# Attention ahead of two expert networks: scores of two heads on the two row halves of TensorE, loads in 4 KB rows, decay on values and result

## The chip, the cores and the metric

The kernel runs on one core of one Trainium2 chip. The metric is the device time of one execution in microseconds (us), less is better. Before the change it was 1580.83 us, the median of three runs (1585.57, 1577.12 and 1580.83).

## What is computed

Three stages follow each other. The first, the only one that the change touches, is a causal attention whose weights decay with distance instead of passing a softmax. The second sends each of the 4608 tokens to one of 8 experts, the third is a dense network.

```python
# q, k, v: (B, H, S, D) = (8, 8, 576, 64), float32
gamma = 1.0 - 2.0 ** (-5.0 - np.arange(H))
rel = pos[:, None] - pos[None, :]
Dmat = np.where(rel >= 0, gamma[:, None, None] ** rel[None], 0.0)
ret = (q @ k.transpose(0, 1, 3, 2)) / np.sqrt(D) * Dmat[None]
x = (ret @ v)                      # -> (B*S, H*D) = (4608, 512)
x = moe(x, ...)                    # argmax over 8 experts, 512 -> 1024 -> 512
out = mlp(x, ...)                  # 512 -> 2048 -> 512, h - tanh(h)
```

The decay gamma^(i-j) is a product of a part of the query's place, gamma^i, and a part of the key's place, gamma^(-j). That is what both versions build on, each in its own way.

## The kernel before

The 4608 tokens are 36 tiles of 128 (`TL`). A sequence has 576 tokens, so 9 tiles (`PERIOD`) hold two sequences and the fifth tile of each nine (t % 9 == 4) holds the end of one and the start of the next, 64 tokens each. All work of one tile is emitted in one pass of a loop over t (L531 on); every engine then runs its own list in that order, and waits by semaphores.

For tile t the pieces are:

- `load_group` (L247): q, k and v of two tiles at once (`LG = 2`), five transfers on SP's queue: the transposed keys `kpad` in two halves of 64 partitions (L255, L256), with each head's half beside zeros, the transposed queries `qt` (L257), the values `vn` (L258) and the keys again, untransposed, `kn` (L259). In memory a partition's row of a tile pair is 1 KB for each head pair of `kT` and `qT`, and 2 KB for each tile of `vN` and `kN`. The buffers hold two groups. A group is ordered two groups ahead, at odd t, once its buffers are free.
- `scores` (L310), emitted for t+1 ahead of `attend` of t: eight matmuls (L318) give the scores of 8 heads; each uses all 128 rows, since the zeros in `kpad` blot out the other head of the pair. VectorE (DVE) multiplies them by a table of decay and causality, `d_full` (L320), into `a`, in two halves of four heads. In the mixed tile GpSimd (POOL) sets a quarter of `a` to zero (L323).
- `scaled` (L326), emitted for t+2: POOL multiplies the queries by gamma^i, `qq` (L331), and the keys by gamma^(-j), `kk` (L335).
- `attend` (L342): `xp` = running state times `qq` (four matmuls, L354) plus `vn` times `a` (eight matmuls on two column halves, L362); then the state in `st` is raised by `kk` times `vn` (eight, column halves, L377). DVE copies one half of the state to `sdiag`, ScalarE (ACT) the other (L383).
- `evac_x` (L386): ACT copies `xp` to `xt` (L390).
- Between these stand, for the group of four tiles before, `route_a`, `route_b` and `route_c` (L417, L426, L448; the routing's logits, argmax and ranks), `scatter` (POOL's indirect writes, L476), and `store_x` (four transposes on TensorE, L487, a scaling on ACT, L492, and a write to `x_d` on ACT's queue).
- `filler` (L507): one of 28 steps that turn seven float64 weight tiles of the third stage to float32 pairs (`conv`, L168, mostly on DVE). The weights' next 512 KB load (L173) is issued on SP's queue from such a step, and waits there until DVE has read the one buffer.

The lines that set the order of the loads:

```python
if t % LG == LG - 1 and t // LG + 2 < NLG:
    load_group(t // LG + 2)
if t + 4 in (5, 6, 7, 8):
    nc.sync.dma_start(out=qs[:, t + 3], in_=A["qs"][t + 3])
```

When the first 28 tiles are routed, `choose` (L392) picks the expert with most of them, and its first unit of 400 tokens is gathered from `x_d` (L164) while the last tiles run. The expert stage begins with the matmuls of L667, and neither it nor the third stage is changed.

Of the kernel before, what the change touches and what calls it, by code (L numbers as in the profile page):

```python
# [8 lines left out]
F32 = mybir.dt.float32  # L9
# [5 lines left out]
ALU = mybir.AluOpType  # L15
# [6 lines left out]
DM = H * D  # L22
E, FF = 8, 1024
DFF = 2048
TL = 128
NTILE = NT // TL
PERIOD = 9
LG = 2
NLG = NTILE // LG
# [18 lines left out]
# -h(h) for small h:  s = (SQ_A u + SQ_B)^2, (s + SQ_C)(u - SQ_R) u h, u = h^2  # L48
# [4 lines left out]
def _consts():  # L53
    g = (1.0 - 2.0 ** (-5.0 - np.arange(H))).astype(np.float64)
    j = np.arange(TL)[:, None]
    i = np.arange(TL)[None, :]
    low = (j <= i)
    rel = np.where(low, i - j, 0)
    dec = np.where(low[None], g[:, None, None] ** rel[None], 0.0) / 8.0
    d_full = np.ascontiguousarray(dec.transpose(1, 0, 2)).astype(np.float32)  # L60
    qs = np.zeros((PERIOD, 2, H // 2, D, TL))
    ks = np.zeros((TL, PERIOD, H))
    for t in range(PERIOD):
        pos = TL * t + np.arange(TL)
        bb, loc = pos // S, pos % S
        start = bb == (TL * t) // S
        for h in range(H):
            if t % PERIOD:
                qs[t, h % 2, h // 2] = (np.where(start, g[h] ** loc, 0.0) / 8.0)[None, :]
            nxt = bb == (TL * (t + 1) - 1) // S  # L70
            ks[:, t, h] = np.where(nxt, g[h] ** (-loc.astype(np.float64)), 0.0)
    qs = np.ascontiguousarray(qs.transpose(0, 1, 3, 2, 4).reshape(PERIOD, 128, H // 2, TL))
    return {
        "d_full": d_full,
        "qs": np.ascontiguousarray(qs[1:]).astype(np.float32), "ks": ks.astype(np.float32),
    }


def _layout(inputs):
    q, k, v = inputs["q"], inputs["k"], inputs["v"]  # L80

    def tr(a):
        a = a.transpose(1, 3, 0, 2).reshape(H // 2, 128, NLG, LG * TL)
        return np.ascontiguousarray(a.transpose(2, 1, 0, 3))

    def tok(a):
        a = a.transpose(0, 2, 1, 3).reshape(NLG, LG, TL, DM)
        return np.ascontiguousarray(a.transpose(0, 2, 1, 3))
# [7 lines left out]
        "qT": tr(q), "kT": tr(k), "kN": tok(k), "vN": tok(v),  # L96
# [11 lines left out]
def kernel(tc, A, out):  # L108
    nc = tc.nc
    with ExitStack() as ctx:  # L110
# [33 lines left out]
        def turn_rows(u, s, src, tp):  # L144
            """Tile s of a unit's rows to a pair of float32r, features on the partitions."""
# [61 lines left out]
        with tc.manual_schedule():  # L207
            make_identity(nc, ident)
            # attention's own buffers on the left; what the routing needs, which ends later, on the right
# [4 lines left out]
            gld = p1("gld", 2)  # L214
# [10 lines left out]
            d_full = att.tile([128, H, TL], F32, name="d_full")  # L225
            qs = att.tile([128, PERIOD - 1, H // 2, TL], F32, name="qs")
            ks = att.tile([128, PERIOD, H], F32, name="ks")
            sdiag = [att.tile([128, H // 2, 128], F32, name=f"sdiag{i}") for i in range(2)]
            wg = const.tile([128, KD, 32], F32, name="wg")
            kpad = [att.tile([128, H // 2, 2, LG * TL], F32, name=f"kpad{i}") for i in range(2)]  # L230
# [14 lines left out]
            gt = {}  # L245

            def load_group(g, parts=1):  # L247
                kp = kpad[g % 2]
                qt = gld.tile([128, H // 2, LG * TL], F32, name="qt")
                vn = gld.tile([128, LG, DM], F32, name="vn")  # L250
                kn = gld.tile([128, LG, DM], F32, name="kn")
                for i in range(parts):
                    c = slice(i * LG * TL // parts, (i + 1) * LG * TL // parts)
                    r = slice(i * LG // parts, (i + 1) * LG // parts)
# [5 lines left out]
                gt[g] = (kp, qt, kn, vn)  # L260

            for i, eng in enumerate((nc.vector, nc.gpsimd)):
                eng.memset(kpad[i][0:64, :, 1, :], 0.0)
                eng.memset(kpad[i][64:128, :, 0, :], 0.0)
# [3 lines left out]
            load_group(0, LG)  # L268
            for i in range(2):
                nc.scalar.dma_start(out=d_full[:, 4 * i:4 * i + 4], in_=A["d_full"][:, 4 * i:4 * i + 4])  # L270
            nc.scalar.dma_start(out=ks, in_=A["ks"])
            nc.scalar.dma_start(out=wg[:, :, 0:E], in_=A["wg"])
            for t in (1, 2):
                nc.sync.dma_start(out=qs[:, t - 1], in_=A["qs"][t - 1])
            nc.scalar.dma_start(out=mid, in_=A["ids"].bitcast(I32).rearrange("p (t w) -> p t w", w=2))
            nc.scalar.dma_start(out=mb.rearrange("p a e -> p (a e)"), in_=A["mb"].to_broadcast([128, 2 * E]))
            load_group(1, LG)
            for t in (3, 4):
                nc.sync.dma_start(out=qs[:, t - 1], in_=A["qs"][t - 1])

# [26 lines left out]
            a_t, q_t, k_t, s_t, x_ps = {}, {}, {}, {}, {}  # L307
            xt = {}

            def scores(t):  # L310
                kp, qt, kn, vn = gt[t // LG]
                c = slice((t % LG) * TL, (t % LG + 1) * TL)
                a = tmp.tile([128, H, TL], F32, name="a")
# [12 lines left out]
            def scaled(t):  # L326
                kp, qt, kn, vn = gt[t // LG]
                c = slice((t % LG) * TL, (t % LG + 1) * TL)
                if t % PERIOD:
                    qq = tmp.tile([128, H // 2, TL], F32, name="qq")  # L330
                    nc.gpsimd.tensor_tensor(out=qq, in0=qt[:, :, c], in1=qs[:, t % PERIOD - 1], op=ALU.mult)  # L331
                    q_t[t] = qq
                if t % PERIOD != PERIOD - 1:
                    kk = tmp.tile([128, H, D], F32, name="kk")
                    nc.gpsimd.tensor_tensor(  # L335
                        out=kk, in0=kn[:, t % LG].rearrange("p (h d) -> p h d", h=H),
                        in1=ks[:, t % PERIOD].unsqueeze(2).to_broadcast([128, H, D]), op=ALU.mult)
                    k_t[t] = kk
# [3 lines left out]
            def attend(t):  # L342
                kp, qt, kn, vn = gt[t // LG]
                r = t % PERIOD
                xp = ps_x.tile([128, H // 2, TL], F32, name="xp")
                a = a_t.pop(t)
                inter = r != 0
                after = not inter or t == NTILE - 1

                def before():  # L350
                    if inter:
                        ss, qq = s_t.pop(t), q_t.pop(t)
                        for p in range(H // 2):
                            nc.tensor.matmul(out=xp[:, p, :], lhsT=ss[:, p, :], rhs=qq[:, p, :],  # L354
                                             start=not after and p == 0, stop=after, skip_group_check=True)
# [3 lines left out]
                for p in range(H // 2):  # L359
                    for s in range(2):  # L360
                        h = 2 * p + s
                        nc.tensor.matmul(out=xp[64 * s:64 * s + 64, p, :], lhsT=vn[:, t % LG, h * D:(h + 1) * D],  # L362
                                         rhs=a[:, h, :], start=after and p == 0, stop=True,
# [4 lines left out]
                if r != PERIOD - 1:  # L368
                    first = r == 0 or r == PERIOD // 2
# [3 lines left out]
                    kk = k_t.pop(t)  # L373
                    for p in range(H // 2):
                        for s in range(2):
                            h = 2 * p + s
                            nc.tensor.matmul(out=st[64 * s:64 * s + 64, p, :], lhsT=kk[:, h], rhs=vn[:, t % LG, h * D:(h + 1) * D],  # L377
                                             start=first and p == 0, stop=True, skip_group_check=True,
                                             tile_position=(0, 64 * s))
# [614 lines left out]
```

## Time and profile before

| | |
|---|---|
| three runs, us | 1585.57, 1577.12, 1580.83 |
| median, us | 1580.83 |
| profiled execution: span of its instructions, us | 1571.7 |
| median less span, us | 9.1 |
| TensorE busy in the whole span | 1457.5 us, 93% |
| DVE, ACT, POOL busy | 1071.6, 704.5, 286.6 us |

For the profiled execution the profile has only its span; the time of the whole execution is not listed apart, and the 9.1 us stand for what lies around the span.

The span is that of one execution, from the first to the last instruction. "Busy" of TensorE is modelled, since matmuls are pipelined: where they follow without a gap, the distance from the start of one group to the start of the next is the better price. The 40 slices of the page are 39.3 us each; attention ends early in the eighth.

### The profile page before, as it was taken

The page shows a single profiled execution, that of the slowest core. Times are in us where ns is not written, and L with a number is a line of the kernel's source. Part 1 is how long each engine was busy: PE and PEld are TensorE (multiplying, and loading weights), DVE is VectorE, ACT ScalarE, POOL GpSimd, SP SyncE. Part 2 cuts the span into 40 slices and gives each one's busy share as a digit, 9 for nine tenths or more (in the row PEclk, how much of TensorE's full clock was granted, in tenths as well). Part 3 has the DMA queues.
Part 4 walks back from the last instruction along what each step waited for, and adds up shares of the span by engine and source line. Part 5 has one row for each costly group of instructions (what it writes and reads, how often), then busy time and mean ns, then how long its engine had stood idle before and what let it go on. Part 6 is the DMA issues. An engine that isn't in the chain of part 4 may idle for free.

```text
span 1571.7 us, 22138 instructions
## 1 busy us (share of the span) xinstructions
PE 1457.5 (93%) x8171; PEld 1279.0 (81%) x8171; DVE 1071.6 (68%) x1775; ACT 704.5 (45%) x1305; POOL 286.6 (18%) x340
## 2 busy tenths in 40 slices
PE   5777777789999999999998999999999999999996
PEld 5666766689999999999776888888888888888885
DVE  3546654457777776774688777877777787877774
ACT  1212222334343344444566555555555555555552
POOL 5234435311111111111232111111111011111101
PEclk8878988999999999999999999999999999999998
DMA  8897797633323522232201000000001000000000
GB/s 234 222 162 166 183 210 147 167 90 117 104 102 117 197 81 78 96 124 88 77 27 59 23 27 27 28 27 28 28 0 37 18 28 27 28 27 1 28 1 27
DMA packets 71008, 127.90 MB, mean 81 GB/s; under 512 B 18704, under 2 KB 37136, under 8 KB 70896
## 3 DMA queue, kind: packets, MB, share of 16 engines
q1 hardware_dynamic: 54976, 92.09, 22.2%
q0 software_dynamic: 7344, 19.44, 3.7%
q10 hardware_dynamic: 8576, 14.91, 3.2%
q8 instruction: 66, 1.08, 0.3%
q14 instruction: 46, 0.38, 0.1%
HBM read 131.10 MB, written 33.09 MB: 104 GB/s over the span
## 4 chain that ended last, share of the span: by engine, by line
PE 39%; issue 6%; DVE 3%; ACT 1%; POOL 1%; DMA 1%; DVEq 0%; POOLq 0%; ACTq 0%
PE hp L667 20%; PE acc L951 7%; PE acc L952 7%; PE acc L953 7%; DVE xl L932 1%; DVE xl L933 1%; DMA o<-wo_d 1%; ACT xh L922 0%; DVE xh L924 0%; POOL out_dram L964 0%; DVE xl L931 0%; DVE lo L927 0%; POOL woutl L905 0%; ACT xh L929 0%; ACT xl L930 0%
## 5 line engine op out<-in xcount | busy, mean ns | idle before, releaser
L951 PE MATMUL acc<-wouth,hi 128*128 128x512 f32 x576 | 226.2, 393 | 4.6 <-ACT o L961 4.6
L667 PE MATMUL hp<-yh,winh 128*128 128x512 f32 x576 | 226.5, 393 | 1.4 <-DVEq L887 1.4
L953 PE MATMUL acc<-wouth,lo 128*128 128x512 f32 x576 | 226.2, 393 | 1.6 <-DVE lo L927 1.6
L667 PE MATMUL hp<-yl,winh 128*128 128x512 f32 x576 | 226.3, 393 | 0.0
L667 PE MATMUL hp<-yh,winl 128*128 128x512 f32 x576 | 226.3, 393 | 0.0
L952 PE MATMUL acc<-woutl,hi 128*128 128x512 f32 x576 | 226.2, 393 | 0.0
L921 ACT ACTIVATE xh<-hp 128x512 f32<-128x512 f32 x144 | 86.1, 598 | 296.9 <-PE hp L667 280.1
L923 DVE TENSOR_TENSOR xl<-xh,hp 128x512 f32<-128x512 f32 x144 | 99.0, 688 | 160.4 <-ACT xh L922 160.4
L767 ACT ACTIVATE hi<-hp 128x400 fp32r<-128x400 f32 x96 | 48.4, 504 | 229.9 <-PE hp L667 229.7
L932 DVE SCALAR_TENSOR_TENSOR xl<-xh,xl 128x512 f32<-128x512 f32 x144 | 135.8, 943 | 15.4 <-DVE xl L931 0.5
L866 PE MATMUL acc<-hi,wh 128*128 128x400 f32 x384 | 137.7, 358 | 5.4 <-ACT wh L742 4.0
L768 DVE SCALAR_TENSOR_TENSOR lo<-hp,hi 128x400 fp32r<-128x400 f32 x96 | 55.0, 573 | 124.9 <-ACT hi L767 122.7
L318 PE MATMUL sc<-qt,kpad 128*128 128x128 f32 x576 | 87.5, 316 | 53.7 <-DMA qt<-in_qT_dram 52.7
L868 PE MATMUL acc<-hi,wl 128*128 128x400 f32 x384 | 133.5, 348 | 0.0
L667 PE MATMUL hp<-xl,wh 128*128 128x400 f32 x384 | 132.8, 346 | 0.0
L667 PE MATMUL hp<-xh,wl 128*128 128x400 f32 x384 | 132.6, 345 | 0.1
L667 PE MATMUL hp<-xh,wh 128*128 128x400 f32 x384 | 132.1, 344 | 0.4 <-ACT wh L742 0.4
L951 PEld LDWEIGHTS acc<-wouth,hi 128*128 128x128 f32 x576 | 108.8, 189 | 29.1 <-ACT o L961 5.0
L867 PE MATMUL acc<-lo,wh 128*128 128x400 f32 x384 | 132.2, 344 | 0.0
L953 PEld LDWEIGHTS acc<-wouth,lo 128*128 128x128 f32 x576 | 108.8, 189 | 28.3 <-DVE lo L927 5.1
L318 PEld LDWEIGHTS sc<-qt,kpad 128*128 128x128 f32 x576 | 82.4, 228 | 60.4 <-issue 45.4
L667 PEld LDWEIGHTS hp<-yh,winh 128*128 128x128 f32 x576 | 108.3, 188 | 25.8 <-PEq L887 1.7
(174 smaller groups left out, 2865.7 us busy)
## 6 DMA issues: line engine op xcount, KB each, us to landing
raw<-in_w_dram SPq DMA_DIRECT2D x91, 512.0 KB
y_d<-yo SPq DMA_DIRECT2D x12, 800.0 KB
yr<-y_d SPq DMA_DIRECT2D x9, 1024.0 KB
raw<-in_wi_dram SPq DMA_DIRECT2D x16, 512.0 KB
kpad<-in_kT_dram SPq DMA_DIRECT2D x32, 256.0 KB
qt<-in_qT_dram SPq DMA_DIRECT2D x16, 512.0 KB
vn<-in_vN_dram SPq DMA_DIRECT2D x16, 512.0 KB
kn<-in_kN_dram SPq DMA_DIRECT2D x16, 512.0 KB
```

What stands on the lines that cost most here:

```text
L318: nc.tensor.matmul(out=sc[:, i, :], lhsT=kp[:, h // 2, h % 2, c], rhs=qt[:, h // 2, c], start=True, stop=True)
L667: nc.tensor.matmul(out=hp, lhsT=lhs, rhs=rhs, start=j == 0, stop=j == 3 * KD - 1)
L768: nc.vector.scalar_tensor_tensor(out=lo, in0=hp, scalar=0.0, in1=hi.bitcast(F32), op0=ALU.max, op1=ALU.subtract)
L866: nc.tensor.matmul(out=o, lhsT=wh[:, cs], rhs=hi, start=first, stop=False)
L867: nc.tensor.matmul(out=o, lhsT=wh[:, cs], rhs=lo, start=False, stop=False)
L868: nc.tensor.matmul(out=o, lhsT=wl[:, cs], rhs=hi, start=False, stop=last)
L921: nc.scalar.activation(out=u, in_=hp, func=ACTF.Square)
L923: nc.vector.tensor_tensor(out=v, in0=u, in1=hp, op=ALU.mult)
L932: nc.vector.scalar_tensor_tensor(out=v, in0=s, scalar=SQ_C, in1=v, op0=ALU.add, op1=ALU.mult)
L951: nc.tensor.matmul(out=acc[s], lhsT=hi[:, c], rhs=wouth[f], start=first, stop=False)
L952: nc.tensor.matmul(out=acc[s], lhsT=hi[:, c], rhs=woutl[f], start=False, stop=False)
L953: nc.tensor.matmul(out=acc[s], lhsT=lo[:, c], rhs=wouth[f], start=False, stop=last)
```

## The change

The loads are laid out anew: `qk` holds queries and keys of a tile, transposed, in one row of 4 KB for each partition, and `vk` values and keys, also 4 KB. A tile is ordered on its own, four tiles ahead (`AHEAD = 4`, four buffers each). `kpad`, its zeros, `d_full` and `qs` are gone.

The scores of a head pair are two matmuls with 64 rows each, one on the rows 0 to 63 and one on 64 to 127, into two banks. They are multiplied by a mask of ones and zeros that all heads share. The mixed tile has a mask of its own, so POOL's memset is gone. The values are scaled by gamma^(-j) on POOL (`vs`), in every tile; queries and keys are used as loaded. The part gamma^i / 8 is applied as `xp` is read out: on DVE, as a product with the table `gx`, where ACT copied before. Both halves of the state are now copied by ACT. In the mixed tile the matmuls of the state run over half the rows or columns.

```diff
-LG = 2
+AHEAD = 4
@@ loads
-                nc.sync.dma_start(out=kp[0:64, :, 0, c], in_=A["kT"][g, 0:64, :, c])
-                (nc.scalar if g + i == 0 else nc.sync).dma_start(out=kp[64:128, :, 1, c], in_=A["kT"][g, 64:128, :, c])
-                nc.sync.dma_start(out=qt[:, :, c], in_=A["qT"][g, :, :, c])
-                nc.sync.dma_start(out=vn[:, r], in_=A["vN"][g, :, r])
-                nc.sync.dma_start(out=kn[:, r], in_=A["kN"][g, :, r])
+            def load_tile(t):
+                qk = gld.tile([128, 2, H // 2, TL], F32, name="qk")
+                vk = gld.tile([128, 2, DM], F32, name="vk")
+                nc.sync.dma_start(out=qk, in_=A["qk"][t])
+                (nc.scalar if t == 0 else nc.sync).dma_start(out=vk, in_=A["vk"][t])
+            def load_gx(r):
+                nc.sync.dma_start(out=gx[:, r], in_=A["gx"][r])
@@ scores
-                for hf in range(2):
-                    sc = ps_sc.tile([128, 4, TL], F32, name="sc")
-                    for i in range(4):
-                        h = 4 * hf + i
-                        nc.tensor.matmul(out=sc[:, i, :], lhsT=kp[:, h // 2, h % 2, c], rhs=qt[:, h // 2, c],
-                                         start=True, stop=True)
-                    nc.vector.tensor_tensor(out=a[:, 4 * hf:4 * hf + 4], in0=sc, in1=d_full[:, 4 * hf:4 * hf + 4], op=ALU.mult)
-                if t % PERIOD == PERIOD // 2:
-                    nc.gpsimd.memset(a[0:64, :, 64:128], 0.0)
+                sc = [ps_sc.tile([128, H // 2, TL], F32, name="sc") for _ in range(2)]
+                for p in range(H // 2):
+                    for s in range(2):
+                        r64 = slice(64 * s, 64 * s + 64)
+                        nc.tensor.matmul(out=sc[s][:, p, :], lhsT=qk[r64, 1, p, :], rhs=qk[r64, 0, p, :],
+                                         start=True, stop=True, tile_position=(64 * s, 0))
+                m = int(t % PERIOD == PERIOD // 2)
+                for s in range(2):
+                    nc.vector.tensor_tensor(out=a[:, s], in0=sc[s], in1=mask[:, m:m + 1, :].to_broadcast([128, H // 2, TL]), op=ALU.mult)
@@ scaled
-                if t % PERIOD:
-                    nc.gpsimd.tensor_tensor(out=qq, in0=qt[:, :, c], in1=qs[:, t % PERIOD - 1], op=ALU.mult)
-                if t % PERIOD != PERIOD - 1:
-                    nc.gpsimd.tensor_tensor(out=kk, in0=kn[...], in1=ks[...], op=ALU.mult)
+                nc.gpsimd.tensor_tensor(out=vs, in0=vk[:, 0]..., in1=vsc[:, t % PERIOD]..., op=ALU.mult)
@@ attend: state to sdiag
-                        (nc.scalar.copy if s else nc.vector.tensor_copy)(out=ss[r64, :, r64], in_=st[r64])
+                        nc.scalar.copy(out=ss[r64, :, r64], in_=st[r64])
@@ evac_x
-                nc.scalar.copy(out=xt[g][:, :, r * TL:(r + 1) * TL], in_=x_ps.pop(t))
+                nc.vector.tensor_tensor(out=xt[g][:, :, r * TL:(r + 1) * TL], in0=x_ps.pop(t), in1=gx[:, t % PERIOD], op=ALU.mult)
@@ loop over t
-                if t % LG == LG - 1 and t // LG + 2 < NLG:
-                    load_group(t // LG + 2)
+                if t + AHEAD < NTILE:
+                    load_tile(t + AHEAD)
+                if t + 3 < PERIOD:
+                    load_gx(t + 3)
```

SP's queue, from the weight load of pass 7 to that of pass 11, before. Rows are DMA issues in the order of the queue, target<-source and the target's shape:

```order
L173 DMA raw<-in_wi_dram 128x1024
L255 DMA kpad_129<-in_kT_dram 64x4x256
L256 DMA kpad_129<-in_kT_dram 64x4x256
L257 DMA qt<-in_qT_dram 128x1024
L258 DMA vn<-in_vN_dram 128x1024
L259 DMA kn<-in_kN_dram 128x1024
L255 DMA kpad_128<-in_kT_dram 64x4x256
L256 DMA kpad_128<-in_kT_dram 64x4x256
L257 DMA qt<-in_qT_dram 128x1024
L258 DMA vn<-in_vN_dram 128x1024
L259 DMA kn<-in_kN_dram 128x1024
L173 DMA raw<-in_wi_dram 128x1024
```

The same stretch of the queue with the change:

```order
L163 DMA raw<-in_wi_dram 128x1024
L239 DMA qk<-in_qk_dram 128x1024
L240 DMA vk<-in_vk_dram 128x1024
L239 DMA qk<-in_qk_dram 128x1024
L240 DMA vk<-in_vk_dram 128x1024
L239 DMA qk<-in_qk_dram 128x1024
L240 DMA vk<-in_vk_dram 128x1024
L239 DMA qk<-in_qk_dram 128x1024
L240 DMA vk<-in_vk_dram 128x1024
L163 DMA raw<-in_wi_dram 128x1024
```

Ten transfers for four tiles have become eight of 512 KB each. The weight load still stands in the same queue, ahead of the loads of its pass. Those of pass 7 were for the tiles 10 and 11 before, and are for tile 11 now; tile 10 is ordered a pass earlier.

DVE's list in the passes 7 and 8 and at the start of 9, before (`a` is the product for the next tile, `cv_` a step of the weight conversion, `sdiag` the copied half of the state):

```order
L320 TENSOR_TENSOR a<-sc,d_full 128x512 x2
L189 TENSOR_SCALAR cv_m<-cv_m 128x512
L190 SCALAR_TENSOR_TENSOR cv_e<-raw,cv_e 128x512
L383 COPY sdiag_126<-st 64x4x64
L320 TENSOR_TENSOR a<-sc,d_full 128x512 x2
L194 TENSOR_TENSOR cv_a<-cv_a,cv_e 128x512
L195 TENSOR_TENSOR cv_a<-cv_a,cv_m 128x512
L320 TENSOR_TENSOR a<-sc,d_full 128x512 x2
L203 TENSOR_TENSOR winl<-cv_a,winh 128x512
```

DVE's list at the same place with the change:

```order
L303 TENSOR_TENSOR a<-sc,mask 128x512 x2
L179 TENSOR_SCALAR cv_m<-cv_m 128x512
L180 SCALAR_TENSOR_TENSOR cv_e<-raw,cv_e 128x512
L366 TENSOR_TENSOR xt<-xp,gx 128x4x128
L303 TENSOR_TENSOR a<-sc,mask 128x512 x2
L184 TENSOR_TENSOR cv_a<-cv_a,cv_e 128x512
L185 TENSOR_TENSOR cv_a<-cv_a,cv_m 128x512
L366 TENSOR_TENSOR xt<-xp,gx 128x4x128
L303 TENSOR_TENSOR a<-sc,mask 128x512 x2
```

The copy of the half state has left DVE's list. The read-out of `xp` has come in at its place, and it stands in every pass, where the state's copy missed the last tile of each nine.

## Rows read from the trace of the kernel before

**Rows 1.** Page, busy tenths of the whole span in 40 slices of 39.3 us: TensorE, its granted clock, mean busy share of the DMA engines.

```profile
PE   5777777789999999999998999999999999999996
...
PEclk8878988999999999999999999999999999999998
...
DMA  8897797633323522232201000000001000000000
```

**Rows 2.** Busy time by stretch: the stretch, its length, busy us (and number of instructions) of TensorE, its weight loads, DVE, ACT and POOL, then granted clock, share of the 16 DMA engines and GB/s. The first row is attention as a whole.

```profile
9.00:279.00 270.00, 202.16 (x2154) 182.78 (x2153) 138.95 (x296) 61.29 (x119) 109.34 (x129) 0.85 0.83 186
218.83:244.28 25.45, 25.15 (x304) 22.58 (x302) 19.12 (x47) 9.74 (x20) 11.19 (x13) 1.00 1.03 232
151.58:169.40 17.82, 15.88 (x195) 14.01 (x193) 14.64 (x32) 5.94 (x12) 7.88 (x9) 1.00 0.80 143
112.50:117.00 4.50, 4.50 (x28) 4.28 (x29) 1.98 (x3) 0.00 (x0) 0.00 (x0) 0.54 1.08 185
119.50:123.00 3.50, 3.50 (x52) 3.38 (x50) 3.40 (x4) 0.81 (x2) 3.31 (x5) 1.00 0.97 371
```

**Rows 3.** Who waited for whom from 9 to 279 us: engine and line <- releaser: us in total, times, longest.

```profile
POOL kk L335 <- DMA kn<-in_kN_dram: 56.8, 11, 12.6
PE sc L318 <- DMA qt<-in_qT_dram: 45.9, 10, 9.9
PE xp L354 <- ACT sdiag L383: 6.1, 5, 3.0
PE m L487 <- ACT xo L492: 3.7, 1, 3.7
PE m L395 <- ACT xo L492: 2.4, 1, 2.4
```

**Rows 4.** DMA traffic: of 9 to 279 us packets and MB with their sizes, and of the stretch 112.5 to 117 us.

```profile
DMA packets 27695, 50.17 MB, mean 186 GB/s; under 512 B 4412, under 2 KB 15215, under 8 KB 27669
...
DMA packets 555, 0.83 MB, mean 185 GB/s; under 512 B 49, under 2 KB 372, under 8 KB 555
```

**Rows 5.** Timeline of the same stretch, SP's queue: start us, length of the issue, line, transfer.

```profile
111.43 0.33 SPq L257 DMA_DIRECT2D qt<-in_qT_dram  x1
118.02 0.33 SPq L258 DMA_DIRECT2D vn<-in_vN_dram  x1
118.45 0.37 SPq L259 DMA_DIRECT2D kn<-in_kN_dram  x1
```

**Rows 6.** Waits of SP's queue from 9 to 279 us: line <- releaser: us in total, times, longest.

```profile
SPq L173 <- DVE sdiag L383: 45.2, 4, 13.5
SPq L258 <- PE st L377: 34.9, 8, 6.2
SPq L257 <- DMA x_d<-xo: 28.4, 7, 8.3
SPq L173 <- DVE cv_e L190: 22.3, 2, 13.3
```

**Rows 7.** Timeline of TensorE in the stretch without load waits, and at the head and the end of the stage (the last row is the first matmul of the experts): start us, us, what, instructions, [idle before].

```profile
6.77 3.75 PE L318 MATMUL sc<-qt,kpad 128*128 128x128 f32 x16 [6.77 <-DMA qt<-in_qT_dram]
12.79 2.44 PE L318 MATMUL sc<-qt,kpad 128*128 128x128 f32 x16 [2.28 <-DMA qt<-in_qT_dram]
15.16 1.98 PE L362 MATMUL xp<-a,vn 128*64 128x128 f32 x16
...
218.83 1.95 PE L318 MATMUL sc<-qt,kpad 128*128 128x128 f32 x16
...
236.19 1.09 PE L362 MATMUL xp<-a,vn 128*64 128x128 f32 x16
237.12 0.64 PE L377 MATMUL st<-vn,kk 128*64 128x64 f32 x16
...
238.17 0.60 PE L487 MATMUL m<-ident,xt 128*128 128x128 f32 x4
238.61 1.95 PE L318 MATMUL sc<-qt,kpad 128*128 128x128 f32 x16
240.40 1.06 PE L354 MATMUL xp<-qq,sdiag 128*128 128x128 f32 x8
...
278.82 1.16 PE L354 MATMUL xp<-qq,sdiag 128*128 128x128 f32 x8
...
292.58 0.45 PE L667 MATMUL hp<-xh,wh 128*128 128x400 f32 x1 [0.37 <-ACT wh L742]
```

**Rows 8.** Groups by line from 9 to 279 us: line, engine, operation, out<-in, shapes, count | busy us, mean ns of one | idle before.

```profile
L320 DVE TENSOR_TENSOR a<-sc,d_full 128x512 f32<-128x512 f32 x72 | 48.3, 685 | 87.6 <-PE sc L318 87.2
L331 POOL TENSOR_TENSOR qq<-qt,qs 128x512 f32<-128x512 f32 x32 | 41.2, 1287 | 67.7 <-DMA qt<-in_qT_dram 51.4 <-PE xp L354 9.3 <-DMA qs<-in_qs_dram 6.6
L335 POOL TENSOR_TENSOR kk<-kn,ks 128x512 f32<-128x512 f32 x32 | 33.5, 1047 | 82.1 <-DMA kn<-in_kN_dram 56.8 <-PE sc L318 18.9 <-PE st L377 6.4
L390 ACT COPY xt<-xp 128x512 f32<-128x512 f32 x35 | 20.5, 585 | 14.5 <-PE xp L362 13.7
L383 DVE COPY sdiag<-st 64x256 f32<-64x256 f32 x32 | 13.2, 414 | 31.6 <-PE st L377 29.6 <-POOL kk L335 1.8 <-issue 0.3
L383 ACT COPY sdiag<-st 64x256 f32<-64x256 f32 x32 | 11.7, 367 | 128.4 <-DVE sdiag L383 124.1 <-DVE cv_m L184 3.4 <-ACT xo L492 0.8
```

**Rows 9.** One line's instructions from 218 to 244 us: engine, operation, duration in ns min/median/max.

```profile
L318 PEld LDWEIGHTS sc<-qt,kpad x80: 186/192/193, 218.7 to 240.2; 128*128 128x128 f32 x80
L318 PE MATMUL sc<-qt,kpad x80: 274/275/377, 218.8 to 240.3; 128*128 128x128 f32 x80
```

More of the change, by code (lines that the diff above doesn't have):

```diff
@@ L56, in _consts @@
     i = np.arange(TL)[None, :]
[L57 to L67, printed above, removed]
-            if t % PERIOD:
[L69 to L72, printed above, removed]
+    low = j <= i
+    mask = np.stack([low, low & ((j < 64) == (i < 64))], axis=1)
+    loc = (TL * np.arange(PERIOD)[:, None] + np.arange(TL)[None, :]) % S
+    up = g[:, None, None] ** loc[None] / 8.0
+    gx = up.reshape(H // 2, 2, 1, PERIOD, TL).transpose(1, 2, 3, 0, 4)
+    gx = np.broadcast_to(gx, (2, D, PERIOD, H // 2, TL)).reshape(128, PERIOD, H // 2, TL)
+    vsc = (g[:, None, None] ** (-loc[None].astype(np.float64))).transpose(2, 1, 0)
     return {
-        "d_full": d_full,
-        "qs": np.ascontiguousarray(qs[1:]).astype(np.float32), "ks": ks.astype(np.float32),
+        "mask": np.ascontiguousarray(mask).astype(np.float32),
+        "gx": np.ascontiguousarray(gx.transpose(1, 0, 2, 3)).astype(np.float32),
+        "vsc": np.ascontiguousarray(vsc).astype(np.float32),
     }
@@ L213 @@
             att = p1("att", 1)
[L214 removed]
+            gld = p1("gld", AHEAD)
             tmp = p1("tmp", 2)
@@ L324, in scores @@
                 a_t[t] = a
             def scaled(t):
[L327 to L330, printed above, removed]
-                    nc.gpsimd.tensor_tensor(out=qq, in0=qt[:, :, c], in1=qs[:, t % PERIOD - 1], op=ALU.mult)
-                    q_t[t] = qq
-                if t % PERIOD != PERIOD - 1:
[L334 to L338, printed above, removed]
+                qk, vk = gt[t]
@@ L347, in attend @@
                 inter = r != 0
-                after = not inter or t == NTILE - 1
+                mid_t = r == PERIOD // 2
+                after = not inter or mid_t or t == NTILE - 1
+                w = TL // 2 if mid_t else TL
                 def before():
                     if inter:
-                        ss, qq = s_t.pop(t), q_t.pop(t)
+                        ss = s_t.pop(t)
                         for p in range(H // 2):
-                            nc.tensor.matmul(out=xp[:, p, :], lhsT=ss[:, p, :], rhs=qq[:, p, :],
+                            nc.tensor.matmul(out=xp[:, p, 0:w], lhsT=ss[:, p, :], rhs=qk[:, 0, p, 0:w],
@@ L360, in attend @@
                     for s in range(2):
-                        h = 2 * p + s
-                        nc.tensor.matmul(out=xp[64 * s:64 * s + 64, p, :], lhsT=vn[:, t % LG, h * D:(h + 1) * D],
-                                         rhs=a[:, h, :], start=after and p == 0, stop=True,
+                        nc.tensor.matmul(out=xp[64 * s:64 * s + 64, p, :], lhsT=vs[:, 2 * p + s],
+                                         rhs=a[:, s, p, :], start=after and p == 0, stop=True,
                                          skip_group_check=True, tile_position=(0, 64 * s))
@@ L368, in attend @@
                 if r != PERIOD - 1:
-                    first = r == 0 or r == PERIOD // 2
+                    first = r == 0 or mid_t
                     if first:
@@ L376, in attend @@
                             h = 2 * p + s
-                            nc.tensor.matmul(out=st[64 * s:64 * s + 64, p, :], lhsT=kk[:, h], rhs=vn[:, t % LG, h * D:(h + 1) * D],
-                                             start=first and p == 0, stop=True, skip_group_check=True,
-                                             tile_position=(0, 64 * s))
+                            nc.tensor.matmul(out=st[64 * s:64 * s + 64, p, :], lhsT=vk[k0:TL, 1, h * D:(h + 1) * D],
+                                             rhs=vs[k0:TL, h], start=first and p == 0, stop=True, skip_group_check=True,
+                                             tile_position=(k0, 64 * s))
                     ss = sdiag[t % 2]
@@ L566 @@
                     load_ids(base, idt0)
-                    x0 = [gld.tile([128, LG, DM], F32, name=n) for n in ("vn", "kn")]
+                    x0 = [gld.tile([128, 2, DM], F32, name="vk") for _ in range(SE // 2)]
                     x0 = [x0[s // 2][:, s % 2] for s in range(SE)]
```

68 lines of the change are left out of this document (28 added, 40 removed).

## The prediction

> **What bounds the kernel now.** The page comes first: TensorE is at nine tenths or more in nearly every slice after the ninth, but at five to seven tenths in the first eight; in the first seven of them the granted clock is mostly below nine tenths and the DMA engines stand at seven to nine tenths [rows 1]. Attention is thus the stage with room, and it is the stage that is changed. The busy time by stretch says how much: over the 270 us from 9 to 279, TensorE is busy 202.16 at a mean clock of 0.85, DVE 138.95, the DMA engines 0.83 of the time at only 186 GB/s [rows 2]. The waits say what ends last: the scores wait 45.9 us for `qt` in ten long waits of up to 9.9 us, POOL 56.8 us for `kn` [rows 3]. After such waits TensorE restarts at the lower of its two levels, 1.2 GHz instead of 2.4: in the stretch from 112.5 to 117 us, behind a load wait, the granted clock is 0.54 [rows 2].
>
> Why do the loads come late? Two things show. First the rate: in that same stretch, behind the issue of `qt` [rows 5], 372 of 555 packets are under 2 KB [rows 4]; the engines are fully busy and move 185 GB/s; from 119.5 to 123 us, behind the issue of `vn` and `kn` with their 2 KB rows, a share of 0.97 moves 371 GB/s [rows 2, 5]. Short rows cost about as much engine time as long ones. Second the lead: SP's queue stands still 45.2 and 22.3 us at the weight load, until DVE has freed its buffer, 34.9 us until `attend` has freed `vn`, and 28.4 us for a store to `x_d` [rows 6], and by the code a group is ordered in pass t for scores that are emitted in pass t + 2.
>
> What TensorE does without load waits is seen from 218.83 to 244.28 us: five tiles in 25.45 us, 25.15 of it busy, clock 1.00 [rows 2, 7]. That is 5.09 us a tile, against (279.98 - 15.16) / 36 = 7.36 us over all 36, counted from the first `attend` to the end of the last [rows 7].
>
> **The change part by part.**
>
> *Loads.* A tile moves the same q, k, k and v, 1.05 MB. With gx (9 x 0.26), seven weight loads (0.52 each) and 28 stores to `x_d` (0.26 each) the stage has 37.7 + 2.4 + 3.7 + 7.3 = 51.1 MB, against 50.17 moved before [rows 4]. At 371 GB/s, a rate of a mixed stretch with 2 KB rows and longer, that is 138 us; at 232 GB/s, the rate of the stretch from 218.83 with the engines full [rows 2], 220 us; at the old 186, 275 us. I take the 138, since no row of the new loads is under 2 KB, and keep 220 as the bad end. The lead grows: a tile is ordered in pass t, when `attend` has freed its buffers, and the scores that use it are emitted in pass t + 3. The longest wait of SP's queue is 13.5 us [rows 6], what three passes of 5 us cover. So the load waits go, and the lower clock that follows them.
>
> *Scores on TensorE.* Sixteen pieces (float32 goes in two) of 128 rows take from 238.61 to 240.40 us, 1.79 us [rows 7]. The trace has no matmul on row halves. The nearest row is that on column halves: sixteen pieces of `xp` out of `a` take from 236.19 to 237.12, 0.93 us, so that two run at once [rows 7]. Bounds: 0.93 us if row halves overlap as column halves do, 1.79 if they don't, and above that if a half's weight load is no longer hidden (a rival below). I take 0.93, from the only row on halves of either kind. That saves 0.86 us a tile: 5.09 - 0.86 = 4.23 us, 152 us for 36. The shorter matmuls of the mixed tile (four of 36 tiles) are left at nothing.
>
> The Trainium skill speaks against this term. "TensorE: Matmul & The Clock Gate", section "LDWEIGHTS (loading the stationary operand)", has the time of a weight load depend on the columns alone and not on the rows; half a load of rows would cost a whole one. By that rule, if the loads of the two halves also queue behind each other, the scores stay at 1.79 us; no run here shows which. That is the second rival, with its time from the rows.
>
> *DVE.* It loses 32 copies of the state, 13.2 us, and gains 36 read-outs of `xp`. The nearest row is L320, a product of PSUM and SBUF of the same 128x512: 685 ns [rows 8], so 24.7 us. The product with the mask keeps L320's price; that the mask is read again for each head is bounded by 685 ns and POOL's 1047 ns for such an operand in `kk` [rows 8], and I take the row of DVE itself. Sum: 138.95 - 13.2 + 24.7 = 150.4 us, 4.18 a tile. DVE comes level with TensorE.
>
> *ACT* drops the copies to `xt` (20.5 us) and takes 32 more state copies of 367 ns, 11.7 us [rows 8]; it was busy 61.29 of 270 [rows 2] and bounds nothing. The wait of TensorE for `sdiag`, 6.1 us in all [rows 3], loses its cause, a DVE copy standing behind other work: ACT now starts at once. Between the end of `st` and the next use of `sdiag` TensorE has the scores, 0.93 us, and in most passes four transposes of 0.44 us (238.17 to 238.61 [rows 7]); two copies take 0.73. What is late next there is ACT itself, when a store to `x_d` holds it.
>
> *POOL* drops `qq`, 41.2 us, and swaps `kk` for `vs` at the same price, 1.05 us x 36 [rows 8]. It is not a bound. `vs` is now needed by `xp` as well as by `st`, but it is made a pass ahead.
>
> *The head of the stage.* The first `attend` starts at 15.16 us, after the second tile's scores at 12.79, which wait for a transfer behind the first tile's and the tables [rows 7]. With the two tiles' `qk` among the first five transfers it lies between 6.8 us (the first scores now, 6.77) and 15.2; I take 10, a gain of 5.
>
> *Sum.* TensorE 152, DVE 150, DMA 138 us: none of the three can run at its floor while it waits for the others. In the dense stretch of before TensorE was 99% busy beside a DVE at 75%; from 151.58 to 169.40, with DVE at 14.64 / 17.82 = 82%, TensorE idled 11% [rows 2]. With both level I add 15% to 152, my choice between these and more: 175 us. To that come 6 us of waits behind `x_d` stores at the choice of the first expert (3.7 + 2.4 [rows 3]), which stay: 181 us, 5.0 a tile. Attention then ends at 10 + 181 = 191 us instead of 280, 89 us sooner. What follows it, the gather and the expert stage at full TensorE, is unchanged and starts as much sooner: 1571.7 - 89 = 1482.7 us of span, and with the 9.1 us around it **1492 us**. The profiled span of 1571.7 plus 9.1 is the median of 1580.83 by this reckoning, so both sides are on one footing.
>
> **The rivals.**
>
> *Row halves do not overlap.* TensorE stays at 5.09 x 36 = 183 us, DVE at 82% of that; with 8% of waits (half of the forecast's, since DVE has room) and the 6 us, 204 us. End at 214, 66 us sooner: 1515. For it: nothing in the trace shows row halves, and the weight loads stand as close as the matmuls (186 and 274 ns, both half hidden [rows 9]). Against it: the column halves.
>
> *The DMA engines stay the bound.* At 232 GB/s the 51.1 MB take 220 us; end at 230, 50 us sooner: 1531. For it: a share of 1.03 at that rate in the very stretch without load waits [rows 2]. Against: its packets include the 1 KB rows that go.
>
> *No change: the queue, not the rows, held the loads.* If the weight load goes on blocking SP's queue for the 67.5 us that it did [rows 6] and the rate stays 186 GB/s, the stage needs its 275 us: 1586 with a head at 10. For it: the load still stands there. Against: four tiles of lead, against a longest wait of 13.5.
>
> *Slower: a row half's weight load is not hidden.* Now a weight load of 186 to 192 ns and a matmul of 275 overlap, so that a piece costs 112 ns of the 1.79 us. If on row halves each load waited for the matmul before and each matmul for its load, sixteen pieces would cost 16 x (192 + 275) = 7.5 us [rows 9], a tile 5.09 - 1.79 + 7.47 = 10.8 us, the stage 388 us: 118 us later, 1699. It decides from a tile of 7.36 us on, that is scores of 1.79 + 2.27 = 4.1 us, over twice what they take. For it: alternating halves was never tried in this trace. Against: alternating column halves do not do it.
>
> **How the numbers follow.** The forecast has 0.61, halves that do not overlap 0.20, DMA as the bound 0.13, no change 0.03, slower 0.03. A measurement of this kernel can tell about 0.5%, 8 us, from no change. Faster by more than that is the sum of the first three, 0.94; within it 0.03; slower 0.03. The forecast's own range: with no loss to waiting and a head at 8 us the stage ends at 160, 120 us sooner, 1461; with 25% lost instead of 15, 1507. The 8-in-10 range runs on to the two rivals of like sign: 1462 to 1535.
>
> **What would show it.** Right: about 0.93 us from the start of a tile's scores to the next group on TensorE; no wait of TensorE for `qk`, DMA over 250 GB/s in attention; granted clock near 1.0 there; DVE busy about 150 us and over 80% of the stage; the first expert matmul near 204 us, where it now follows the end of attention by 12.6 us (292.58 [rows 7]). Wrong: scores still 1.8 us apart (second rival), load waits on `qk` with the engines full (third) or idle (fourth), waits of TensorE for DVE of over a us in most passes, which would put the time above 1507.

## The result, and the profile after

The changed kernel takes 1527.49 us, the median of four runs (1524.81 to 1531.44). The kernel before, run beside it, takes 1579.70 (1577.12 to 1585.57). The ratio is 0.966, with a 95% interval of 0.963 to 0.969: 52 us sooner. 1492 was forecast, with 1462 to 1535 as the range; the time lies inside it only because the range runs on to the rivals: the forecast's own range ended at 1507. It is the time of the third rival, DMA engines that stay the bound (1531).

The page of the changed kernel, to be held against [rows 1]:

```profile
PE   7787877899999999999998999999999999999996
...
PEclk9899978999999999999999999999999999999998
DMA  8999955232235222441210000000000010000000
GB/s 338 206 234 231 230 124 176 89 113 97 99 124 202 79 72 72 140 141 24 83 56 28 28 28 1 28 28 29 28 28 29 0 35 21 28 28 0 29 1 28
```

Attention now ends in the sixth slice instead of the eighth. Inside it TensorE is at seven and eight tenths instead of five to seven, still not at nine, and the DMA engines stand at eight and nine in the first five slices. Only the first slice, 38 us, has a rate near the forecast one.

Busy time by stretch (length; busy us and instructions of PE, PEld, DVE, ACT, POOL; granted clock; DMA share; GB/s), against [rows 2]:

```profile
9.00:230.00 221.00, 175.75 (x2149) 148.55 (x2147) 129.76 (x300) 54.17 (x116) 71.98 (x97) 0.89 0.90 223
...
50.00:150.00 100.00, 76.39 (x937) 64.08 (x930) 61.75 (x142) 25.08 (x53) 33.13 (x45) 0.90 1.01 219
```

Full DMA engines that move 219 GB/s, and TensorE busy three quarters of the time: the loads bind.

Its waits from 9 to 230 us, against [rows 3] (us in total, times, longest):

```profile
POOL vs L309 <- DMA vk<-in_vk_dram: 98.9, 23, 10.2
ACT xo L468 <- DMA x_d<-xo: 76.7, 20, 8.0
...
PE sc L299 <- DMA qk<-in_qk_dram: 23.6, 11, 6.6
PE m L463 <- ACT xo L468: 16.0, 7, 6.8
...
PE xp L331 <- ACT sdiag L359: 0.7, 1, 0.7
```

TensorE still waits for loads, now 23.6 us instead of 45.9 [rows 3], and behind stores to `x_d` 16.0 us in seven waits instead of 3.7 in one.

TensorE's timeline (start, length, line, output <- inputs), against [rows 7]:

```profile
104.81 1.16 PE L299 MATMUL sc<-qk 64*128 64x128 f32 x16 [0.67 <-DMA qk<-in_qk_dram]
105.90 1.16 PE L331 MATMUL xp<-qk,sdiag 128*128 128x128 f32 x8
...
226.16 1.16 PE L331 MATMUL xp<-qk,sdiag 128*128 128x128 f32 x8
236.52 1.97 PE L144 MATMUL sc<-ident,vk 128*128 128x128 f32 x8 [9.20 <-DMA vk<-x_d,idt]
...
242.78 0.70 PE L643 MATMUL hp<-xh,wh 128*128 128x400 f32 x1
```

The sixteen pieces of a tile's scores now take 105.90 - 104.81 = 1.09 us (1.79 before). Attention ends at 227.3 us instead of 280, the first expert matmul starts at 242.78 instead of 292.58: the gain of the run is made by there.

The stage's DMA between 50 and 150 us, in 40 slices of 2.5 us:

```profile
DMA  9935899399899979697998949998999799968979
GB/s 331 36 23 43 306 338 70 42 365 320 202 221 333 222 231 116 198 243 118 388 326 107 179 95 411 328 188 217 255 344 152 181 421 246 112 108 234 321 115 288
DMA packets 7490, 21.94 MB, mean 219 GB/s; under 512 B 1245, under 2 KB 1245, under 8 KB 7479
```

This is not a steady rate that is too low. Slices at 320 to 421 GB/s alternate with twelve slices under 120, in eight of which the engines are still six to nine tenths busy: packets are on the way and end late. The 10 us from 50 to 60, in 40 slices of 0.25 us, hold the first such stretch:

```profile
DMA  9878999999900000003990010900019099542314
GB/s 229 229 238 312 394 426 393 410 467 213 115 0 0 0 0 0 0 33 131 82 16 0 0 66 33 33 0 0 33 49 66 33 82 82 16 33 49 16 16 33
```

### The profile page after: what moved, and what is told of

It is laid out like the page before. It is cut to its first block, busy times and chain, and to the rows that moved or that the text cites. A ratio compares the mean times of both kernels' runs of the same rounds, so it can differ in the third digit from the quotient of the medians.

```text
span 1523.5 us, 21984 instructions
## 1 busy us (share of the span) xinstructions
PE 1433.4 (94%) x8171; PEld 1246.4 (82%) x8171; DVE 1061.5 (70%) x1777; ACT 696.7 (46%) x1301; POOL 247.3 (16%) x306
## 4 chain that ended last, share of the span: by engine, by line
PE 41%; issue 6%; DVE 5%; ACT 1%; POOL 1%; DMA 0%; DVEq 0%; POOLq 0%; ACTq 0%
PE hp L643 20%; PE acc L927 7%; PE acc L928 7%; PE acc L929 7%; DVE xl L908 1%; DVE xl L909 1%; DVE xh L900 1%; ACT xh L898 1%; DVE xl L907 1%; DVE lo L903 1%; POOL out_dram L940 0%; DMA o<-wo_d 0%; DVE xl L899 0%; POOL woutl L881 0%; ACT xh L905 0%
## 5 line engine op out<-in xcount | busy, mean ns | idle before, releaser
L643 PEld LDWEIGHTS hp<-yh,winl 128*128 128x128 f32 x576 | 108.2, 188 | 24.7
L643 PEld LDWEIGHTS hp<-yl,winh 128*128 128x128 f32 x576 | 108.2, 188 | 24.0
```

The costliest lines, as they stand in the source:

```text
L643: nc.tensor.matmul(out=hp, lhsT=lhs, rhs=rhs, start=j == 0, stop=j == 3 * KD - 1)
```

## The experiments

In this stage POOL issues, once a pass from pass 7 on, a scatter of 128 four-byte words (a tile's token numbers, to `slot_d`), and ACT, from pass 6 on, a 256 KB store to `x_d`. The first store is issued at 46.4 us and the first scatter at 47.4; the trace has the 32 packets of that scatter, and those of a store, between 50 and 53 us, and the rate breaks at 52.75. From 53 to 60 us only 55 packets end, all of loads, 32 GB/s. **Theory S**: the scatter holds loads up. **Theory W**: the store does. **Theory R**: the loads have a rate of 225 GB/s by themselves, as the third rival says. All fourteen kernels, with DMA rate and share between 50 and 150 us and the start of the first expert matmul; each ratio is to the kernel before as it ran beside that kernel, with medians of 1576.1 to 1579.7 us:

| kernel | median, us | ratio to before (95%) | GB/s | share | expert at, us |
|---|---|---|---|---|---|
| before | 1579.7 | 1 | 178 | 0.84 | 292.6 |
| the change | 1527.5 | 0.966 (0.963 to 0.969) | 219 | 1.01 | 242.8 |
| latescat | 1499.5 | 0.951 (0.948 to 0.955) | 304 | 0.88 | 219.8 |
| scat2 | 1562.8 | 0.990 (0.987 to 0.993) | 163 | 1.03 | 289.9 |
| store2 | 1557.7 | 0.988 (0.984 to 0.992) | 210 | 1.04 | 276.1 |
| byhalf | 1533.2 | 0.973 (0.969 to 0.978) | 217 | 1.01 | 249.6 |
| scat64 | 1451.1 | 0.919 (0.915 to 0.922) | 313 | 0.86 | 187.2 |
| before_latescat | 1551.6 | 0.984 (0.980 to 0.988) | 240 | 0.73 | 262.5 |
| late_rows | 1494.6 | 0.946 (0.942 to 0.950) | 303 | 0.95 | 218.7 |
| late_ahead2 | 1581.7 | 1.004 (1.001 to 1.006) | 201 | 0.58 | 299.1 |
| before_scat64 | 1519.4 | 0.961 (0.958 to 0.965) | 208 | 0.66 | 254.9 |
| scat64_byhalf | 1462.6 | 0.926 (0.923 to 0.930) | 294 | 0.81 | 197.1 |
| line4 | 1462.6 | 0.926 (0.922 to 0.929) | 308 | 0.84 | 196.4 |
| scat32 | 1461.1 | 0.925 (0.922 to 0.928) | 316 | 0.86 | 192.7 |

**latescat**: the scatters later.

```diff
-                    for w in due(t - RG - 3):
+                    ws = due(t - RG - 3)
+                    if t < 31:
+                        ws = range(6 * (t - 27), 6 * (t - 26)) if t >= 27 else []
+                    for w in ws:
                         scatter(w)
```

> The scatters of the first 24 tiles (POOL's writes of 128 four-byte words to slot_d) are taken out of passes 7 to 30 and issued six a pass in passes 27 to 30, after nearly all loads are ordered; the result is the same. Theory S (a load's packets stand still for some us behind each scatter): between 50 and 150 us the DMA engines move over 300 GB/s instead of 207 and 231, the waits for qk and vk nearly go, attention ends 20 to 35 us sooner: 1492 to 1510 us. Theory W (they stand still behind the 256 KB stores to x_d) and theory R (the loads' own rate is 225 GB/s, whatever else runs): still 207 to 231 GB/s and 1527 us within 8.

Measured: 1499.5 us and 304 GB/s, as S has it; W and R, which had the rate stay, fall, since neither the stores nor the loads were touched. Its row from 50 to 150 us:

```profile
50.00:150.00 100.00, 94.82 (x1264) 78.57 (x1262) 83.18 (x182) 34.94 (x74) 32.46 (x39) 1.00 0.88 304
```

TensorE goes from 76.39 to 94.82 us busy, at a clock of 1.00, and the engines are no longer full.

**scat2**: each scatter of the first 28 tiles a second time, into `slot2_d`.

```diff
+                if t < EARLY * RG:
+                    apart("slots2", nc.gpsimd.indirect_dma_start(
+                        out=slot2_d[:, :], out_offset=bass.IndirectOffsetOnAxis(ap=pos_s[:, t:t + 1], axis=0), ...))
```

> Every scatter of the first 28 tiles is issued a second time, to a table that nobody reads: 28 more DMAs of 128 words and 28 us more of POOL, spread over 28 passes in which POOL is busy under 3 us. Theory S: each pass has a second stall of 2 to 4 us: 50 to 110 us later, 1580 to 1640. Theories W and R: 1527 us within 8.

Measured: 35 us later and 163 GB/s. The sign is S's; the size is under its 50 to 110: 35 / 28 = 1.3 us a scatter, where the length of the stalls had let me expect 2 to 4.

**store2**: each store a second time, into `x2_d`.

```diff
+                if not spare:
+                    nc.scalar.dma_start(out=x2_d[t * TL:(t + 1) * TL, :], in_=xo)
```

> Every store to x_d that leaves on ACT's queue is issued a second time, to a tensor that nobody reads: 7.3 MB more, in rows of 2 KB. Theory W: a second stall in each pass, 50 to 110 us later, 1580 to 1640. Theory S: only the bytes, 7.3 MB at 371 GB/s, 20 us, or at 225 GB/s 33 us: 1540 to 1560. Theory R: the bytes at 225 GB/s, 33 us: 1560.

Measured: 30 us later. That is the price of 7.3 MB at some 240 GB/s, so the bytes alone; W's second stall did not come.

**byhalf**: the order of the score matmuls.

```diff
-                for p in range(H // 2):
-                    for s in range(2):
+                for s in range(2):
+                    for p in range(H // 2):
```

> The eight score matmuls of a tile are issued four of the lower row half first and then four of the upper, instead of in turns. If the 1.09 us of a tile's scores come of two row halves at work at once, the scores go back to about 1.8 us, 0.7 us a tile or 25 us of TensorE; where the loads set the pace that is partly hidden: 1530 to 1550 us. If a matmul on 64 rows is short by itself, the scores stay at 1.09 us and the time at 1527 within 8.

```profile
102.56 1.71 PE L299 MATMUL sc<-qk 64*128 64x128 f32 x16
104.20 1.16 PE L331 MATMUL xp<-qk,sdiag 128*128 128x128 f32 x8
```

Measured: 1.64 us a tile in place of 1.09, so the gain does come of two row halves at once, and depends on alternating them. The time, 6 us more, has an interval that touches the change's.

**scat64**: a table with 64 bytes for each entry, so that the scatters can stay in their passes (the zeroing and the readers of the table, and `tok_d`, which is copied from it, follow suit).

```diff
-        slot_d = dram.tile([NSLOT, 1], I32, name="slot_d")
+        slot_d = dram.tile([NSLOT, 16], I32, name="slot_d")
-            nc.gpsimd.iota(tokid, pattern=[[TL, NTILE]], ...)
+            nc.gpsimd.iota(tokid, pattern=[[TL, NTILE], [0, 16]], ...)
-                    in_=tokid[:, t:t + 1], in_offset=None))
+                    in_=tokid[:, t], in_offset=None))
```

> The scatters stay in their passes, one a tile, but each token's entry in slot_d is a row of 16 equal words, 64 bytes, instead of one of 4 (the table is 2.4 MB and is zeroed whole at the start, 2.2 MB more in the first 40 us; readers take the first word of a row). Theory S4 (it is the four-byte write that holds the loads up): the stalls go, over 300 GB/s between 50 and 150 us, 1485 to 1505 us, since no late burst delays the choice of the expert as in latescat. Theory S (any scatter holds them up, whatever its width): 219 GB/s between 50 and 150 us as in the change, 1527 to 1540.

Measured: 1451.1 us, below what S4 gave, 76 us under the change and 125 under the kernel before that ran beside it: the version to use. Its DMA from 50 to 150 us:

```profile
DMA  3599999559999945899999369998687999999957
GB/s 138 97 398 416 402 399 404 216 152 399 406 400 368 327 183 146 276 342 368 414 406 361 125 138 393 405 367 296 248 272 254 295 366 417 375 321 389 345 211 280
DMA packets 10752, 31.29 MB, mean 313 GB/s; under 512 B 1446, under 2 KB 1782, under 8 KB 10738
```

Where the rate is under 200 GB/s now, the share is at three to six tenths too: few loads are under way there, instead of loads that stand.

**before_latescat**: the diff of latescat, made to the kernel before.

> The kernel before, with the scatters of the first 24 tiles issued six a pass in passes 27 to 30, as in latescat; all else is as before. If scatters held its loads up as they do in the changed kernel: over 230 GB/s in place of 186 over the stage, 20 to 45 us sooner, 1532 to 1557. If the short rows of its loads were the limit, as the prediction has it: 186 GB/s still, 1577 within 8.

Measured: 1551.6 us and 240 GB/s at a share of 0.73, against 178 at 0.84: the scatters held the old loads up too, with their short rows.

**late_rows**: latescat with the old row sizes (the arrays in memory are laid out to match).

```diff
-                nc.sync.dma_start(out=qk, in_=A["qk"][t])
+                nc.sync.dma_start(out=qk....rearrange("p (c x) -> p c x", c=4), in_=A["qk"][t].rearrange("c p x -> p c x"))
-                (...).dma_start(out=vk, in_=A["vk"][t])
+                (...).dma_start(out=vk, in_=A["vk"][t].rearrange("c p x -> p c x"))
```

> latescat with the row sizes of the kernel before: qk in rows of 1 KB (four pieces a partition) and vk in rows of 2 KB, the same bytes, buffers and order. If short rows cost engine time as the prediction says (185 GB/s where 1 KB rows were the bulk): a tile's 1.05 MB take 4.4 us or more against a pass of 4.4 us, loads wait again, 1505 to 1525 us. If the size of the row counts for little: as latescat, 1499 within 8.

```profile
DMA packets 20737, 30.31 MB, mean 303 GB/s; under 512 B 1178, under 2 KB 12059, under 8 KB 20724
```

Measured: 1494.6 us; over twice as many packets at the same rate as latescat (9948 packets, 304 GB/s). Rows of 1 and 2 KB cost engine time, a share of 0.95 instead of 0.88, but at this rate no wall time.

**late_ahead2**: latescat with two buffers; the load of t + 2 stands ahead of `scaled(t + 2)`.

```diff
-AHEAD = 4
+AHEAD = 2
```

> latescat with two buffers instead of four: a tile is ordered in pass t when its buffers come free, and used by POOL and by the scores of the next pass. If the lead is needed as the prediction says (loads 2.8 us at full rate, plus the weight load's wait of up to 6.5 us on the queue): waits for qk in most passes, 1515 to 1560 us. If the load rate alone was the matter: 1499 within 8.

```profile
PE sc L297 <- DMA qk<-in_qk_dram: 50.6, 19, 6.1
```

Measured: 1581.7 us, later than the range given. With engines busy 0.58 of the time TensorE waits 50.6 us for `qk` from 9 to 200 us, and 85.7 us in 26 waits up to the end of the stage (9 to 290 us): a lead of two tiles instead of four costs 5% of the time, some 80 us, all that the change and the later scatters gain. (The kernel before, with groups of two tiles ordered two groups ahead, lies between the two in its lead.)

**before_scat64**: the diff of scat64, made to the kernel before.

> The kernel before with entries of 64 bytes in slot_d, as in scat64; nothing else changes. If its low load rate of 186 GB/s came from the four-byte scatters: load waits nearly go, 50 to 80 us sooner, 1496 to 1526 us, and the changed kernel's margin over it (scat64 at 1451) is then 45 to 75 us. If it came from its rows or its short lead: 1550 to 1577.

```profile
PE sc L321 <- DMA qt<-in_qT_dram: 30.7, 9, 5.4
```

Measured: 1519.4 us, as expected, but load waits do not nearly go: 30.7 us are left, at a DMA share of 0.66. With engines that are a third idle, that part of the old waits is put down to the lead and not to the rate; no run gave the kernel before a longer lead alone. Without the stalls the change is worth 68 us, from 1519 to scat64's 1451, instead of 52. Those 30.7 us of load waits are the largest part of it that shows; the overlap of the scores is worth some 11 (next), and the rest is not split.

**scat64_byhalf**: byhalf's diff, made to scat64.

> scat64 with the score matmuls of a tile issued half by half, as in byhalf. There the scores took 1.64 us in place of 1.09; here TensorE is busy 99% from 50 to 100 us, so that 36 x 0.55 = 20 us should all show: 1471 us. If VectorE, busy 90% there, is as much the limit: under 10 us, 1451 to 1460.

Measured: 1462.6 us, 11 more and neither of the two values. Attention itself is 11.7 us longer, 176.5 (15.94 to 192.49) against 164.8 (16.17 to 181.0): TensorE's busy time in it grows by 15.8 us, and its idle time falls from 6.7 to 2.7. So some 4 us of the price are hidden by waits that it has anyway.

**line4**: scat64's table, of which a scatter writes the first word of each 64 bytes.

```diff
+                nc.vector.tensor_scalar(out=pos_s[:, gs], in0=pos_s[:, gs], scalar1=4, scalar2=None, op0=ALU.logical_shift_left)
-                    out=slot_d[:, :], out_offset=...
+                    out=slot_d.rearrange("n (w o) -> (n w) o", o=1), out_offset=...
-                    in_=tokid[:, t], in_offset=None))
+                    in_=tokid[:, t, 0:1], in_offset=None))
```

> scat64's table with one entry in each 64 bytes, but only its first word written: 128 writes of four bytes a scatter, each to a place 64 bytes from the next, with one short VectorE operation for each four tiles that multiplies the positions by 16. If a write of four bytes by itself holds loads up: 219 GB/s between 50 and 150 us, 1525 to 1545 us. If it is that neighbouring words of one stretch of 64 bytes are written by several DMA engines at once: 1451 to 1465, as scat64.

```profile
DMA packets 10676, 30.79 MB, mean 308 GB/s; under 512 B 1790, under 2 KB 1790, under 8 KB 10661
```

Measured: 1462.6 us and 308 GB/s. The same number of four-byte writes for each tile, and the rate of scat64: a four-byte write alone does not hold loads up. In the old table the tokens of a tile that go to one expert have consecutive places, here they lie 64 bytes apart; the table is also 16 times as large, and the two are not told apart (see the end).

**scat32**: rows of 32 bytes.

> scat64 with rows of 8 words, 32 bytes. If 32 bytes are written whole: 1445 to 1455 us, a little under scat64 for the smaller table to be zeroed. If a write must be 64 bytes to leave loads alone: over 1500.

Measured: 1461.1 us, 316 GB/s: 32 bytes apart is enough. line4 and scat32 end 10 us behind scat64, with ratios whose intervals touch its own; between 50 and 150 us the three are alike. The end of attention and the routing of the last tiles, in line4, scat32 and scat64:

```profile
183.50 1.16 PE L334 MATMUL xp<-qk,sdiag 128*128 128x128 f32 x8 [1.33 <-issue]
...
192.04 1.93 PE L399 MATMUL m<-xt,wg 128*32 128x512 f32 x8 [5.97 <-DVE xt L369]
...
188.29 1.93 PE L399 MATMUL m<-xt,wg 128*32 128x512 f32 x8 [5.74 <-DVE xt L369]
...
183.73 1.06 PE L399 MATMUL m<-xt,wg 128*32 128x512 f32 x8
```

The profiled spans are 8.4 (line4) and 6.7 us (scat32) longer than scat64's, and the first expert matmul is already 9.2 and 5.5 us later. In both TensorE waits nearly 6 us for DVE's last read-out of `xp`, and does the routing at 1.93 us instead of 1.06; scat64 has no such wait. What held DVE there is not shown.

## Why the prediction was right and wrong

*Loads: the step that failed.* "At 371 GB/s, a rate of a mixed stretch with 2 KB rows and longer, that is 138 us": the stage moved 223 GB/s and took 217 us (10.30 to 227.3). The step rested on the reading of [rows 2, 4, 5] that short rows make the engines slow. late_rows shows that they cost some share of the engines (0.95 instead of 0.88) but not the rate: 303 GB/s with the old rows, once the scatters are out of the way. In the kernel before, too, loads stood behind scatters: before_latescat moves 240 GB/s with the same rows. How much of the one stretch at 185 GB/s is owed to the scatter whose packets lie in it and just before it (111 to 115 us) is not split. The prediction names the scatters nowhere. What would have shown it are slices of 2.5 us instead of means, here of the kernel before from 50 to 150 us:

```profile
DMA  9930396699999995699898998989920036999999
GB/s 224 395 154 3 112 21 48 64 241 315 403 291 254 102 38 29 52 390 87 56 95 205 235 182 284 232 148 288 386 90 0 0 111 72 161 115 243 374 363 237
```

A cost of the row's length would be steady, and this one comes and goes: 38 GB/s at full engines a few slices after 403. In the change the stage took 36 us more than the 181 forecast: TensorE waits 23.6 us for loads and 17.0 behind stores, where 6 were forecast, and its granted clock is 0.89 instead of near 1.0.

*The third rival* had the right time, since it took the old dense stretch's 232 GB/s for what loads get at full engines, which holds as long as the scatters stay. That its 220 us came so near to the measured 217 is luck: it gave no cause, and R, its plain reading, fell with latescat.

*Lead: right.* Without it the gain is gone (late_ahead2), and it is, as far as the waits tell, what the old kernel still lacks in before_scat64. "So the load waits go" failed by the stalls: eleven waits were left.

*Scores: mechanism right, size off.* Row halves overlap (byhalf), but at 1.09 us and not 0.93. The second rival's rule from "TensorE: Matmul & The Clock Gate" in the Trainium skill, by which the scores would have stayed at 1.79, did not decide. The same page has, in its section "🎯 Why this matters for your kernels", that matmuls on distinct row groups run concurrently; 1.09 against 1.64 us agrees, and I had passed over it.

*DVE: prices right, sum wrong.* Groups of instructions on DVE and ACT of the changed kernel from 9 to 230 us (count | busy us, mean ns | idle before):

```profile
L303 DVE TENSOR_TENSOR a<-sc,mask 128x512 f32<-128x512 f32 x70 | 45.0, 684 | 55.9 <-PE sc L299 53.1 <-issue 2.8
L366 DVE TENSOR_TENSOR xt<-xp,gx 128x512 f32<-128x512 f32 x36 | 24.7, 686 | 13.1 <-PE xp L338 10.3 <-PE xp L331 2.9
...
L359 ACT COPY sdiag<-st 64x256 f32<-64x256 f32 x64 | 23.5, 367 | 50.6 <-PE st L353 44.9 <-ACT xo L468 2.7 <-PE m L405 2.1
...
L410 DVE TENSOR_TENSOR lg<-lg,bias 128x32 f32<-128x32 f32 x8 | 1.8, 228 | 0.3
L417 DVE SCALAR_TENSOR_TENSOR cd<-lg,riota 128x32 f32<-128x32 f32 x8 | 1.5, 192 | 0.3
L444 DVE TENSOR_TENSOR cum<-cum,co 128x8 bf16<-128x8 bf16 x8 | 1.3, 167 | 0.3
```

The product with the mask and the read-out cost 684 and 686 ns, 685 forecast; ACT's copies 367, as forecast. But DVE is busy 129.8 us, not 150.4. The same three small routing operations took, in the kernel before:

```profile
L441 DVE SCALAR_TENSOR_TENSOR cd<-lg,riota 128x32 f32<-128x32 f32 x8 | 6.2, 780 | 0.3
...
L468 DVE TENSOR_TENSOR cum<-cum,co 128x8 bf16<-128x8 bf16 x8 | 4.7, 588 | 0.3
L434 DVE TENSOR_TENSOR lg<-lg,bias 128x32 f32<-128x32 f32 x8 | 4.6, 581 | 0.3
```

These three alone lose 10.9 us of busy time; POOL, which ran `qq` beside them, is busy 72 us instead of 109. The Trainium skill's "SBUF — State Buffer", section "Who interferes with whom", has a DVE operation with two inputs from SBUF contend with a GpSimd operation that reads SBUF; these rows agree, but no run here took the neighbour away alone.

*Head, mutual waiting, stores.* The first `attend` starts at 10.30 us, 10 forecast. What the loads hid, scat64 shows. Attention there lasts from 16.17 (TensorE waits 5.65 us for `vs` of POOL, which issues the zeroing of the larger table until 15.0) to 181.0, 164.8 us, where 181 were forecast:

```profile
178.80 1.09 PE L341 MATMUL xp<-a,vs 128*64 128x128 f32 x16
179.83 1.16 PE L334 MATMUL xp<-qk,sdiag 128*128 128x128 f32 x8
187.15 0.45 PE L646 MATMUL hp<-xh,wh 128*128 128x400 f32 x1 [0.26 <-ACT wh L721]
```

With 1.09 us for the scores instead of 0.93 a tile's floor is 4.23 + 0.16 = 4.39 us, 158 for 36, so waiting adds 4% and not 15%, and the waits behind stores, 17 us in the change, shrink to 1.1: those too came of the scatters. The forecast for all but the loads was thus somewhat too slow. scat64's first expert matmul, at 187 us, is 56 us ahead of the change's, and its time 76; some 15 of the other 20 lie behind that matmul (1523.5 - 242.8 against 1452.4 - 187.2 us of span). Of these 7.6 come after TensorE's last matmul (14.4 us to the end of the span against 6.8); neither they nor the rest are explained.

## What to carry to other kernels

A DMA share near 1 says that packets are under way, not what holds them: look at the rate in slices of a few us, and if it alternates between full and nearly nothing, ask which small transfer began just before, and move or widen that one alone. Entries that are scattered word by word are worth a try at 32 bytes apart or more. Longer rows gained no time here, at some 300 GB/s; ordering loads earlier did.

## What the runs showed of the hardware

- Scatters of 128 four-byte words to neighbouring places, half a KB of data each, took the DMA from 304 (latescat) to 219 GB/s over 100 us, and held up loads and stores on other queues. The same writes 64 bytes apart (308 GB/s) and rows of 32 bytes (316 GB/s) did not. "DMA: Bandwidth & Descriptors" in the Trainium skill, section "Specifications", says that writes under 512 bytes are read, changed and written; line4's, as short as before, cost nothing that shows, so shortness is not the whole of it. Whether it is the neighbours in one stretch or the smaller table that matters was not told apart: the table grew from 0.15 to 2.4 MB with the spacing, and to 1.2 in scat32.
- Sixteen score pieces on alternating row halves took 1.09 us, half by half 1.64; sixteen pieces of `xp` on column halves took 0.93 [rows 7].
- Loads in rows of 1 and 2 KB ran at 303 GB/s, in rows of 4 KB at 304, for a share of 0.95 and 0.88.
